# Attention ahead of a mixture of four dense branches: the first batch's head pairs one by one, a load moved, products of two pairs joined, and a planner's durations changed

## The chip, the cores and the metric

The kernel runs on one core of one Trainium2 chip. The metric is the device time of one execution in microseconds (us); below, "the median" is that of several runs. A core has a matrix engine (PE, whose weight loads are listed as PEld), a vector engine (DVE), a scalar engine (ACT), a general engine (POOL), and an engine that issues transfers (SP). They run side by side and wait for each other through semaphores; each executes its own list of instructions in order. Results of PE go to PSUM, which has eight banks of 128 x 512 numbers of four bytes; all else lies in SBUF.

## The reference

Everything is in float32. There are 8 batches, 8 heads, 576 rows and 64 columns to a head; the second half has N = 4608 rows, D = 512, four branches and F = 1024.

```python
kv = einsum('bhsd,bhse->bhde', k, v)          # 64 x 64 for each head
out = einsum('bhsd,bhde->bhse', q, kv)
x = out / sqrt(mean(out * out, -1) + 1e-6) * g_norm
x = x.transpose(0, 2, 1, 3).reshape(4608, 512)
p = domain_probs / (domain_probs.sum(-1, keepdims=True) + 1e-9)
result = sum(p[:, e:e + 1] * (maximum(x @ w1[e], 0) @ w2[e]) for e in range(4))
```

## The kernel before, in words

**Tiling.** The rows of x are cut into nine chunks of 512: the first 512 rows of each of the eight batches, and a ninth that gathers the 64 remaining rows of each batch. Branch e and chunk c make step s = 9e + c, 36 steps in all. A step's `up` makes the hidden layer (x times w1, then the maximum with 0), its `down` multiplies that by w2 and adds to the output. Both use Strassen-like schemes with seven products in place of eight (L868 for up; L1082 and, in most steps of branches 1 to 3, L1157 for down), so DVE, POOL and ACT form many sums and differences. The first step's `up` alone is plain (`up_plain`, L955): 32 products of 128 x 128 by 128 x 512, in four banks of kinds u1 and u2, two sweeps over the halves of the hidden layer.

**Attention of one batch** (`attention`, L570 to L741) goes by head pairs, four to a batch, two to a group. For a pair: q is loaded (two transfers of 128 KB), k and v (288 KB each); PE turns q by four transposes (L616), ACT copies it out (L621); PE multiplies k by v for both heads (L629: 12 products of 96 x 64 by 96 x 64, that is 24 steps on PE, since a float32 product takes two). For a group: ACT copies the k times v of two pairs (L638); PE multiplies q by it ("attend", L651: 64 steps, 64 x 64) into two raw banks, which are of kind db for batches 0 and 1 and of kind ab from batch 2 on. `scaled` (L518) then takes the rows' norm: ACT squares both banks (L533), DVE sums (L540), POOL scales and takes the power -1/2 (L547, L551), DVE multiplies the raw banks by that (L560). PE turns the resulting x (L670, four transposes to a pair), and ACT copies it out times `gcol`, the g_norm weights (L677). Products on 96 x 64 or 64 x 64 use half of PE's array. The 64 remaining rows of all four pairs follow in one go (L695, L712, L725, L735).

**What orders the work.** Nothing is in the program's order. Every operation is put into a `Plan` with a key (its due place in the sequence of steps), a cost (the engines that may do it, with a duration each; DVE or POOL for the sums of `combine`, L360), and what it reads and writes. `layout` (L81) then plays all engines against one clock: PE and SP take the first ready operation in order of key, the others the most urgent; buffers and banks are given out as they come free. A transfer's end is reckoned on a common bus (`bus`). Where PE could do nothing while the first key of its list is below 0, it is given a filler, two transposes of the identity (`idle`, L1289 to L1291). What comes out is one fixed list to each engine; the chip executes these lists with semaphores, whatever the durations turn out to be.

The g_norm weights are loaded by two transfers that stand in the code ahead of the planned ones (L1297), so they are the first on SP's queue. The SP order after them is: q, k, v of pairs 0 to 3 of batch 0, then the four quarters of w1 (512 KB each), then batch 1.

Of the kernel before, what the change touches and what calls it, by code (L numbers as in the profile page):

```python
# [9 lines left out]
ACT = mybir.ActivationFunctionType  # L10
# [24 lines left out]
class Plan:  # L35
# [45 lines left out]
    def layout(self, slots, later, idle, idle_banks, idle_until):  # L81
# [22 lines left out]
        busy = {e: 0.0 for e in todo}  # L104
        bus = port = 0.0
        lanes = [0.0] * self.LANES
        t = 0.0
# [123 lines left out]
def kernel(  # L231
# [104 lines left out]
    def pe(products, columns, passes=2):  # L336
        return {"PE": passes * products * (0.008 + 0.0008125 * columns) + 0.003}

    def dve(n):
        return {"DVE": 0.185 + 0.00104 * n}  # L340

    def act(n):
        return {"ACT": 0.19 + 0.00088 * n}

    def either(n):
        return {"DVE": 0.185 + 0.00104 * n, "POOL": 0.15 + 0.00225 * n}

# [170 lines left out]
    def scaled(key, name, raw, n, x, blocks):  # L518
# [36 lines left out]

        plan.add(key - 0.3, {"POOL": 2.1}, power, reads=[ss], writes=[ss, rt])
        for r in range(2):
# [12 lines left out]
    def attention(b, key, span, rem):  # L570
# [6 lines left out]
        at = lambda j: key + span * j / (NPAIR + 1)  # L577
        kv = [Buf("kvbd", f"kvc{b}_{g}") for g in range(2)]
        qTs = {}

# [23 lines left out]

        for g in range(2):
            kbank = Buf("ab", f"kv{b}_{g}")
            for o in range(2):
                hp = 2 * g + o
                kt, vt, qt = load_pair(hp)
                bank = Buf("ab", f"qT{b}_{hp}")  # L610
                qT = qTs[hp] = Buf("small", f"qT{b}_{hp}")

                def turn(eng, bank=bank, qt=qt):
                    for r in range(NR):
                        rs = slice(r * P, (r + 1) * P)
                        nc.tensor.transpose(bank.ap[:, rs], qt.ap[:, rs], ident[:])  # L616

                plan.add(at(hp), pe(4, P, 1), turn, reads=[qt], writes=[bank])
                plan.add(
                    at(hp), act(NT),  # L620
                    lambda eng, bank=bank, qT=qT: nc.scalar.activation(  # L621
                        out=qT.ap[:], in_=bank.ap[:], func=ACT.Copy),
                    reads=[bank], writes=[qT],
                )

                def key_values(eng, bank=kbank, kt=kt, vt=vt, o=o):
                    for j in range(KR):
                        for r in range(2):
                            nc.tensor.matmul(  # L629
                                bank.ap[r * D:(r + 1) * D, o * D:(o + 1) * D],  # L630
                                lhsT=kv_rows(kt)[:, r, j, :], rhs=kv_rows(vt)[:, r, j, :],
                                start=(j == 0), stop=(j == KR - 1), skip_group_check=True,
                            )

                plan.add(at(hp), {"PE": 0.87}, key_values, reads=[kt, vt], parts=[kbank])
            plan.add(
                at(2 * g + 1), act(P),
                lambda eng, bank=kbank, to=kv[g]: nc.scalar.activation(  # L638
                    out=to.ap[:], in_=bank.ap[:, 0:P], func=ACT.Copy),
                reads=[kbank], writes=[kv[g]],  # L640
            )
            raw = [Buf("ab" if b > 1 else "db", f"raw{b}_{g}_{r}") for r in range(2)]

            def attend(eng, raw=raw, g=g):
                for o in range(2):
                    for i in range(NR):
                        for c in range(2):
                            for r in range(2):
                                half = slice(r * D, (r + 1) * D)
                                at = i * P + c * D  # L650
                                nc.tensor.matmul(  # L651
                                    raw[r].ap[c * D:(c + 1) * D, (o * NR + i) * D:(o * NR + i + 1) * D],
                                    lhsT=qTs[2 * g + o].ap[half, at:at + D],
                                    rhs=kv[g].ap[half, o * D:(o + 1) * D],
                                )

            plan.add(
                at(2 * g + 1.4), {"PE": 1.0}, attend, reads=[qTs[2 * g], qTs[2 * g + 1], kv[g]],
                writes=raw,
            )  # L660
            x = Buf("big", f"xg{b}_{g}")
            scaled(at(2 * g + 1.4), f"{b}_{g}", raw, P, x, 2 * NR)
            for o in range(2):
                hp = 2 * g + o
                bank = Buf("ab" if b > 1 else "db", f"xT{b}_{hp}")

                def turn_x(eng, bank=bank, x=x, o=o):
                    for r in range(NR):
# [3 lines left out]

                plan.add(at(2 * g + 2 + 0.4 * o), pe(4, P, 1), turn_x, reads=[x], writes=[bank])
                xh = x_halves(b)[g]
                plan.add(
                    at(2 * g + 2 + 0.4 * o), act(NT),
                    lambda eng, bank=bank, xh=xh, kt=o: nc.scalar.activation(  # L677
                        out=xh.ap[:, kt * NT:(kt + 1) * NT], in_=bank.ap[:], func=ACT.Copy,
                        scale=gcol[:]),
                    reads=[bank], parts=[xh],  # L680
                )
# [26 lines left out]
        def attend_rem(eng):  # L708
            for hp in range(NPAIR):
                for r in range(2):  # L710
                    half = slice(r * D, (r + 1) * D)
                    nc.tensor.matmul(  # L712
                        rawr[r].ap[0:REM, hp * D:(hp + 1) * D],
                        lhsT=qTr.ap[half, hp * REM:(hp + 1) * REM],
                        rhs=kv[hp // 2].ap[half, hp % 2 * D:(hp % 2 + 1) * D],
                    )

        plan.add(at(NPAIR), {"PE": 0.55}, attend_rem, reads=[qTr] + kv, writes=rawr)
        xr = Buf("small", f"x{n}")
# [222 lines left out]
    def up_plain(s, e, c, key, span):  # L942
# [4 lines left out]
        for i in range(8):  # L947
            uh, a, u = i // 4, i // 2 % 2, i % 2
            bank = Buf("u1" if a == 0 else "u2", f"up{s}_{i}")
            for dh in range(2):  # L950
                w, low = corners[uh, dh]

                def product(eng, w=w, bank=bank, dh=dh, ut=2 * a + u):
# [7 lines left out]
                op = plan.add(  # L961
                    key + span * i / 8 - (1.1 if i < 4 and dh == 0 else 0.0), pe(2, NT), product,
                    reads=[w, low, xh[dh]], **({"parts": [bank]} if dh else {"writes": [bank]}),
# [23 lines left out]
    def result(s, e, c, base):  # L987
# [33 lines left out]
        def merge(key, src, ap, i, half, fresh):  # L1021
# [4 lines left out]
            if fresh and not again:  # L1026
                plan.add(
                    key, act(HN),
                    lambda eng: nc.scalar.activation(  # L1029
# [14 lines left out]
        def send(key, i):  # L1044
# [4 lines left out]
            def fn(eng):  # L1049
# [6 lines left out]
            plan.add(  # L1056
                key, {"POOL": 0.9 * len(where)} if e and not again else {"SP": 0.55 * len(where)},
                fn, reads=[part[i, 0], part[i, 1]] + ([was] if was else []), writes=[now], kb=256,
# [197 lines left out]


    attention(0, -2.0, 1.3, 0.1)
    sums_1 = weights_1(0, -2.5, 0.02, 0.3)
# [35 lines left out]
    with tc.manual_schedule(engines={ENG.PE, ENG.DVE, ENG.Activation, ENG.Pool, ENG.SP}):  # L1295
        for i in range(P // D):
            nc.sync.dma_start(out=gcol[i * D:(i + 1) * D, :], in_=g_norm.unsqueeze(1))  # L1297
        make_identity(nc, ident[:])
# [45 lines left out]
```

## Time and profile before

| | us |
|---|---|
| median of six runs (1741.33 to 1745.49) | 1742.67 |
| the profiled execution | 1740.68 |
| its span, first to last instruction | 1738.7 |

| stretch of the span | PE busy | DVE busy | ACT busy | POOL busy | DMA share |
|---|---|---|---|---|---|
| 0 to 29 us | 24.02 | 2.58 | 6.58 | 3.82 | 0.98 |
| 29 to 37 us | 8.00 | 3.51 | 1.09 | 5.43 | 1.13 |
| 37 to 60 us | 23.00 | 19.03 | 9.81 | 9.27 | 0.80 |
| 60 to 100 us | 40.00 | 29.26 | 19.86 | 25.92 | 0.74 |
| 100 to 200 us | 100.00 | 59.79 | 50.52 | 36.15 | 0.51 |
| 200 to 420 us | 220.00 | 116.89 | 108.07 | 71.92 | 0.41 |
| 420 to 1710 us | 1289.92 | 910.79 | 718.12 | 542.88 | 0.43 |
| 1710 to 1738.7 us | 24.04 | 9.24 | 2.98 | 5.82 | 0.43 |

The page's first part gives the busy time of each engine and the number of its instructions. "Busy" counts fillers as well as work, and ends of PE's instructions are modelled. A row of the waits view has the engine and tile that waited, its line, what it waited for, and then the total in us, the number of times and the longest. A line of the timeline has a start, a length, engine, line, what is written and read, shapes, how many instructions stand together, and in brackets the idle time ahead and who ended it. The chain of waits is followed back from the last instruction; its pieces follow each other without a gap, so their lengths add up to the span. Lines are those of the kernel before; L360 and the like are lines of helpers that issue many operations.

### The profile page before, as it was taken

The numbers are of one execution on the slowest core, as the hardware profiler recorded it, in microseconds if no ns is written. First come the engines' busy times: TensorE is split into PE (matmuls) and PEld (weight loads), VectorE is DVE, ScalarE is ACT, GpSimd is POOL, SyncE is SP. The second block draws the span as 40 slices with busy tenths as digits, with TensorE's granted clock in tenths as the row PEclk, the third lists the DMA queues.
The fourth block names the chain that finished last, engine by engine and source line by source line (L and its number), as shares of the span: only waits on it lengthen the run. The fifth ranks groups of instructions, "written<-read, shape, count | busy, mean of one in ns | idle before, by whom it ended". The sixth has DMA issues, their size and how long they took to land.

```text
span 1738.7 us, 37793 instructions
## 1 busy us (share of the span) xinstructions
PE 1729.0 (99%) x15080; PEld 1650.7 (95%) x15080; DVE 1151.1 (66%) x1745; ACT 917.0 (53%) x2234; POOL 701.2 (40%) x684
## 2 busy tenths in 40 slices
PE   8999999999999999999999999999999999999998
PEld 6699999999999999999999999999999999999998
DVE  2765554556574467777786567777786567777774
ACT  2454544454444455666655456666555446665662
POOL 2633343333333524333356524333345625333331
PEclk9999999999999999999999999999999999999999
DMA  9755544533333333444455434444456434444442
GB/s 229 242 177 159 174 143 128 150 135 127 146 125 107 103 97 105 110 110 110 133 159 134 110 97 110 110 110 110 108 158 160 110 98 110 110 110 109 109 100 49
DMA packets 148592, 220.89 MB, mean 127 GB/s; under 512 B 49600, under 2 KB 90816, under 8 KB 148416
## 3 DMA queue, kind: packets, MB, share of 16 engines
q1 hardware_dynamic: 133312, 191.21, 34.5%
q0 software_dynamic: 15104, 27.27, 11.0%
q8 instruction: 118, 1.93, 0.4%
q14 instruction: 58, 0.48, 0.1%
HBM read 145.30 MB, written 73.14 MB: 126 GB/s over the span
## 4 chain that ended last, share of the span: by engine, by line
PE 99%; DMA 0%; DVE 0%; issue 0%; SPq 0%; ACT 0%
PE u L868 45%; PE db L1082 17%; PE db L1157 16%; PE ab L1157 10%; PE ab L1082 4%; PE u L955 2%; PE ab L629 2%; PE ab L616 1%; PE ab L651 1%; PE ab L1291 1%; PE ab L670 1%; PE db L651 0%; PE ab L712 0%; DMA small<-in_q_dram 0%; PE db L670 0%; PE ab L695 0%
## 5 line engine op out<-in xcount | busy, mean ns | idle before, releaser
L868 PE MATMUL u<-xf,big 128*128 128x128 f32 x3536 | 509.3, 275 | 0.0
L360 DVE TENSOR_TENSOR big<-big,big 128x1024 f32<-128x1024 f32 (+1 forms) x420 | 462.2, 1112 | 56.0 <-ACT big L851 26.1
L868 PEld LDWEIGHTS u<-xf,big 128*128 128x128 f32 x3536 | 456.2, 192 | 4.3
L868 PE MATMUL u<-xf,w1y 128*128 128x128 f32 x2652 | 383.0, 276 | 0.0
L895 DVE TENSOR_TENSOR big<-u,snap 128x256 f32<-128x256 f32 x446 | 188.2, 422 | 257.3 <-PE u L868 192.8
L868 PEld LDWEIGHTS u<-xf,w1y 128*128 128x128 f32 x2652 | 342.1, 192 | 3.7
L887 ACT ACTIVATE snap<-u 128x256 f32<-128x256 f32 x490 | 187.5, 383 | 241.7 <-PE u L868 202.9
L1082 PE MATMUL db<-big,big 128*128 128x256 f32 x1192 | 280.4, 380 | 0.0
L1082 PEld LDWEIGHTS db<-big,big 128*128 128x128 f32 x1192 | 216.3, 190 | 24.5
L360 POOL TENSOR_TENSOR big<-big,big 128x256 f32<-128x256 f32 (+1 forms) x125 | 161.0, 1302 | 162.0 <-DVE big L360 62.1
L887 ACT ACTIVATE big<-u 128x256 f32<-128x256 f32 x446 | 170.1, 383 | 106.2 <-PE u L868 77.3
L360 POOL TENSOR_TENSOR big<-big 128x512 f32<-128x512 f32 (+1 forms) x75 | 90.9, 1213 | 161.6 <-DVE big L360 107.6
L851 ACT ACTIVATE big<-big 128x1024 f32<-128x1024 f32 x124 | 130.1, 1051 | 6.7 <-DVE big L360 4.8
L1157 PE MATMUL db<-big,big 128*128 128x128 f32 x788 | 113.0, 275 | 0.0
L1223 POOL TENSOR_TENSOR big<-big 128x512 f32<-128x512 f32 x19 | 24.1, 1268 | 217.9 <-DVE big L360 164.1
L1185 ACT ACTIVATE snap<-db 128x256 f32<-128x256 f32 (+1 forms) x168 | 59.9, 356 | 94.5 <-PE db L1157 88.1
L887 ACT ACTIVATE u<-u 128x256 f32<-128x256 f32 x245 | 91.0, 371 | 29.1 <-PE u L868 12.4
L1157 PEld LDWEIGHTS db<-big,big 128*128 128x128 f32 x788 | 100.3, 192 | 0.0
L1029 ACT ACTIVATE big<-db,p_all 128x256 f32<-128x256 f32 x90 | 42.6, 473 | 108.9 <-PE db L1082 108.9
L1052 POOL DMA_DIRECT2D out_dram<-big x98 | 88.5, 989 | 22.0 <-ACT big L1029 16.3
L1157 PE MATMUL db<-kv,big 128*128 128x128 f32 x624 | 88.6, 275 | 0.0
L1157 PE MATMUL ab<-kv,big 128*128 128x128 f32 x588 | 84.1, 275 | 0.0
(208 smaller groups left out, 2623.5 us busy)
## 6 DMA issues: line engine op xcount, KB each, us to landing
xf<-x SPq DMA_DIRECT2D x108, 512.0 KB, 3.5
out_dram<-big POOLq DMA_DIRECT2D x82, 256.0 KB, 5.3
xf<-x_h SPq DMA_DIRECT2D x81, 256.0 KB, 3.0
xf<-x SPq DMA_DIRECT2D x81, 256.0 KB, 3.1
x<-xf SPq DMA_DIRECT2D x36, 512.0 KB, 3.0
big<-in_moe_w_dram SPq DMA_DIRECT2D x28, 512.0 KB, 5.2
small<-in_q_dram SPq DMA_DIRECT2D x72, 128.0 KB, 3.9
kv<-in_k_dram SPq DMA_DIRECT2D x30, 288.0 KB, 3.3
```

The source lines that it names most:

```text
L360: lambda eng: adder(eng).tensor_tensor(out=out_(), in0=a(), in1=b(), op=op),
L629: nc.tensor.matmul(bank.ap[r * D:(r + 1) * D, o * D:(o + 1) * D], lhsT=kv_rows(kt)[:, r, j, :], rhs=kv_rows(vt)[:, r, j, :], start=(j == 0 ...
L851: lambda eng: nc.scalar.activation(out=b.ap[:], in_=b.ap[:], func=ACT.Relu),
L868: nc.tensor.matmul(ps.ap[:, u * P:(u + 1) * P], lhsT=w1f[e][m][mm][1]()[:, u * P:(u + 1) * P], rhs=views[m][mm][1](), start=(mm in (1, 5) ...
L887: lambda eng: nc.scalar.activation(out=where(), in_=ps.ap[:, 0:HN], func=ACT.Copy),
L895: lambda eng: nc.vector.tensor_tensor(out=block(whole, a, t), in0=src.ap[:, 0:HN], in1=add_.ap[:], op=ALU.add),
L955: nc.tensor.matmul(bank.ap[:], lhsT=two(w.ap[:])[:, kt, ut * P:(ut + 1) * P], rhs=two(xh[dh].ap[:])[:, kt, :], start=(dh == kt == 0), stop ...
L1029: lambda eng: nc.scalar.activation(out=cell(i, half), in_=ap(), func=ACT.Copy, scale=prob()),
L1052: nc.gpsimd.dma_start(out=dst, in_=cell(i)[parts, :], accum_op=ALU.add)
L1082: nc.tensor.matmul(ps.ap[:, 0:HN], lhsT=four(h[m])[:, kt // 2, t, kt % 2, :], rhs=w2f[e][m].ap[:, kt * HN:(kt + 1) * HN], start=(m in (1, ...
L1157: nc.tensor.matmul(ps.ap[:, o * P:(o + 1) * P], lhsT=b.ap[:, col:col + P], rhs=w2q[e][m][mm][1]()[:, kt, :], start=(mm in (1, 5) and o == ...
L1185: lambda eng: nc.scalar.activation(out=where(), in_=group_of(ps.ap), func=ACT.Copy),
```

## The change

- The eight banks and all products stay. In batch 0 the groups of attention are single pairs: four groups in place of two, each with its own copy of k times v, attend (32 steps), squares, sum, power (8 columns instead of 16), scaling, and turn. One raw bank of each is now of kind db, the other of kind u2. Batches 1 to 7 keep groups of two pairs.
- `key_values` is one operation for a group: the 24 steps of each of its pairs follow one another.
- The loads of g_norm become a planned operation (`load_gains`) with a key between those of pairs 1 and 2; the copies of batch 0's x wait for it.
- x is turned in ab banks in all batches (before: db for batches 0 and 1).
- `up_plain` puts the first half of the products of two banks ahead of their key, not of four.
- The planner's durations: DVE 0.155 in place of 0.185, ACT 0.155 in place of 0.19 (the part per column stays); POOL's power 0.3 + 0.37 for each block in place of 2.1; the first merge of an output cell 0.48 in place of 0.415; POOL's sends 1.0 in place of 0.9; k times v 0.73 a pair + 0.2, attend 0.5 a pair + 0.2, the remainder's attend 0.75 in place of 0.55. The common bus starts at 3.0 in place of 0.

The lines of the changed kernel are 4 to 18 higher from there on: L616 becomes L620, L629 L634, L638 L647, L651 L660, L670 L678, L677 L686, L955 L968, L868 L881, L1082 L1095, L1291 L1311.

```diff
-        bus = port = 0.0
+        bus, port = 3.0, 0.0
...
     def dve(n):
-        return {"DVE": 0.185 + 0.00104 * n}
+        return {"DVE": 0.155 + 0.00104 * n}
...
     def act(n):
-        return {"ACT": 0.19 + 0.00088 * n}
+        return {"ACT": 0.155 + 0.00088 * n}
...
-        plan.add(key - 0.3, {"POOL": 2.1}, power, reads=[ss], writes=[ss, rt])
+        plan.add(key - 0.3, {"POOL": 0.3 + 0.37 * blocks}, power, reads=[ss], writes=[ss, rt])
...
-        for g in range(2):
-            kbank = Buf("ab", f"kv{b}_{g}")
-            for o in range(2):
-                hp = 2 * g + o
+        groups = ((0,), (1,), (2,), (3,)) if b == 0 else ((0, 1), (2, 3))
+        for g, pairs in enumerate(groups):
+            n = f"{b}_{g}"
+            kbank = Buf("ab", f"kv{n}")
+            kv = Buf("kvbd", f"kvc{n}")
+            held = []
+            for o, hp in enumerate(pairs):
+                kvs[hp] = kv, o
                 kt, vt, qt = load_pair(hp)
+                held.append((kt, vt))
...
-                def key_values(eng, bank=kbank, kt=kt, vt=vt, o=o):
+            def key_values(eng, bank=kbank, held=held):
+                for o, (kt, vt) in enumerate(held):
                     for j in range(KR):
...
-                plan.add(at(hp), {"PE": 0.87}, key_values, reads=[kt, vt], parts=[kbank])
+            size = len(pairs)
...
+            plan.add(
+                at(pairs[-1]), {"PE": 0.73 * size + 0.2}, key_values,
+                reads=[t for ts in held for t in ts], writes=[kbank],
+            )
...
-            raw = [Buf("ab" if b > 1 else "db", f"raw{b}_{g}_{r}") for r in range(2)]
+            raw = [Buf(("db", "u2")[r] if b == 0 else "ab" if b > 1 else "db", f"raw{n}_{r}") for r in range(2)]
...
-                at(2 * g + 1.4), {"PE": 1.0}, attend, reads=[qTs[2 * g], qTs[2 * g + 1], kv[g]],
-                writes=raw,
-            )
-            x = Buf("big", f"xg{b}_{g}")
-            scaled(at(2 * g + 1.4), f"{b}_{g}", raw, P, x, 2 * NR)
-            for o in range(2):
-                hp = 2 * g + o
-                bank = Buf("ab" if b > 1 else "db", f"xT{b}_{hp}")
+                at(pairs[-1] + 0.4), {"PE": 0.5 * size + 0.2}, attend,
+                reads=[qTs[hp] for hp in pairs] + [kv], writes=raw,
+            )
+            x = Buf("big", f"xg{n}")
+            scaled(at(pairs[-1] + 0.4), n, raw, P, x, size * NR)
+            for o, hp in enumerate(pairs):
+                bank = Buf("ab", f"xT{b}_{hp}")
...
-                    reads=[bank], parts=[xh],
+                    reads=[bank] + ([gains] if b == 0 else []), parts=[xh],
...
-                    key + span * i / 8 - (1.1 if i < 4 and dh == 0 else 0.0), pe(2, NT), product,
+                    key + span * i / 8 - (1.1 if i < 2 and dh == 0 else 0.0), pe(2, NT), product,
...
+    gains = Buf(None, "gains", gcol)
+
+    def load_gains(eng):
+        for i in range(P // D):
+            nc.sync.dma_start(out=gcol[i * D:(i + 1) * D, :], in_=g_norm.unsqueeze(1))
+
+    plan.add(-2.85, {"SP": 1.1}, load_gains, writes=[gains], kb=1)
     attention(0, -2.0, 1.3, 0.1)
...
-        for i in range(P // D):
-            nc.sync.dma_start(out=gcol[i * D:(i + 1) * D, :], in_=g_norm.unsqueeze(1))
         make_identity(nc, ident[:])
```

## The prediction

> **What bounds the kernel now.** I read the page first, then the waits of PE, then PE in order of time over the first 40 us, then the chain of waits inside the attention stage.
>
> The page:
> ```profile
> span 1738.7 us, 37793 instructions
> PE 1729.0 (99%) x15080; PEld 1650.7 (95%) x15080; DVE 1151.1 (66%) x1745; ACT 917.0 (53%) x2234; POOL 701.2 (40%) x684
> ```
> PE is busy for all but 9.7 us. The waits view of PE, for the whole span, says where (us, times, longest):
> ```profile
> PE ab L1291 <- POOL ident masks.py:199: 1.3, 1, 1.3
> PE ab L616 <- DMA small<-in_q_dram: 1.3, 1, 1.3
> PE ab L1291 <- issue: 1.3, 1, 1.3
> PE ab L1291 <- ACT small L621: 0.7, 1, 0.7
> PE db L651 <- issue: 0.3, 1, 0.3
> ```
> All of these lie before 29 us; the rest is the end of the span, about 4.6 us after the last product. From 29 us on PE never waits. So only three things change the time: when PE stops doing filler, how much PE work there is, and any new PE wait. But busy is not useful: L1291 is filler (transposes of the identity that the planner puts where PE would idle). Lines from PE's timeline:
> ```profile
> 1.35 4.10 PE L1291 MATMUL ab<-ident 128*128 128x128 f32 x18 [1.35 <-POOL ident masks.py:199]
> 6.77 0.63 PE L616 MATMUL ab<-ident,small 128*128 128x128 f32 x4 [1.31 <-DMA small<-in_q_dram]
> 7.23 2.13 PE L1291 MATMUL ab<-ident 128*128 128x128 f32 x18
> ...
> 28.96 7.13 PE L955 MATMUL u<-big,big 128*128 128x512 f32 x16
> 35.94 1.04 PE L1291 MATMUL ab<-ident 128*128 128x128 f32 x8
> 36.81 1.04 PE L670 MATMUL db<-ident,big 128*128 128x128 f32 x8
> ```
> The last filler ends at 36.8 us, where the x of the last two head pairs is turned. After that PE runs useful work without a gap. The first 18 transposes take 4.10 us (0.213 each), the next 18 take 2.13 us with the last one's drain in it (0.109 each): PE starts at half speed.
>
> The chain of waits in the attention stage has a second cost (start, us, what):
> ```profile
> 122.90 1.73 PE db L1082 x8
> 124.63 0.89 PE u L868 x8
> 125.52 0.85 PE ab L629 x24
> 126.37 2.43 PE u L868 x20
> 128.80 0.44 PE ab L616 x4
> 129.24 0.85 PE ab L629 x24
> 130.09 1.53 PE u L868 x12
> ```
> Eight L868 cost 0.89 (0.1115 each), so 20 should cost 2.23 and 12 should cost 1.34. After a block of L629, which uses half of the array, they cost 0.20 more. Between starts of instructions I read the same: the step into a half-array block is 0.205 instead of 0.112 (0.094 more), its last step 0.1 longer, and the first step of the full-size work behind it 0.10 longer (0.057 if that is transposes). One such block between full-size work costs 0.29.
>
> **The change part by part**, against the profiled execution (1740.68 us, span 1738.7). That is 2.0 below the median of the six runs, 1742.67.
>
> Start-up. I take PE's order from the instruction lists of both programs.
> - Before the first q transpose there are now 30 filler transposes instead of 18. The g_norm loads leave the head of SP's queue (two issues, 1.23 us), so q lands near 5.4 instead of 6.63, but PE is still in its filler. By about 5.3 us 18 slow ones are done; 12 more at 0.109 end near 6.65 (earliest 6.5; 7.75 if all 30 run slow). Before: 6.77. So the 1.27 us that every load of pairs 0 and 1 gains buys 0.1.
> - From there to the turn of the last pair's x: filler 84 x 0.109 = 9.2; four q turns 1.75; twelve x turns 1.3; four k-times-v blocks at 0.85+0.094+0.057 = 4.0; four half-length attends at 0.73 = 2.9 (half of the 64 steps, the three penalties); four 512-column products (x16 in 6.9, so 0.86 each) 3.45. Sum 22.6, so the last x turn starts at 29.2.
> - Nothing waits in it: the k and v of pair 3 land at 20.2 in the old trace and are wanted at 20.4; for pair 3 the squares, sum, power and scaling end 4.5 us after attend (old, two pairs: 7.0, of it 2.9 the power and 1.22 the sum, both by width), and 6 us of PE work stand there. If that cover were gone, each us late is a us.
> - Before, this point was at 36.81. By then before had done four more products (3.45) and had four more transposes left (0.44), so after owes 3.0. **Gain 36.8 - 29.2 - 3.0 = 4.6.**
>
> Fewer changes of the array's shape. Counted in the lists after the start: 65 half-array blocks before, 62 of them entered from full-size work; now 52 and 46, since k times v of two pairs runs as one block in seven batches. 16 x 0.294 = 4.7, less three more joints of half-array blocks with each other at 0.1: **gain 4.4.** The work itself is the same instructions.
>
> What batch 1 pays. Its raw results still lie in the two db banks, and the list now shows the first L1082 product (into a db bank) only 1.72 + 0.7 + 3.1 = 5.6 us of PE work behind the second attend: two 512-column products, the remainder's attend, seven L868 pairs. The bank is free when DVE has scaled the raw result. In the old trace this took 9.0 us (66.87 to 75.84), and PE had other work there. The lines of POOL and DVE:
> ```profile
> 68.11 1.22 DVE L540 TENSOR_REDUCE ss<-big 128x16 f32<-128x1024 f32 x1 [0.88 <-ACT big L533]
> 70.82 2.90 POOL L551 TENSOR_TENSOR rt<-ss,mhalf 128x16 f32<-128x16 f32 x1
> 73.76 1.29 DVE L560 TENSOR_TENSOR big<-db,rt 128x512 f32<-128x512 f32 x2
> ```
> In the new lists POOL does a 1024-wide sum of the hidden layer (2.4) ahead of that power; it starts after the last relus, 2.75 behind the attend. 2.75 + 2.4 + 3.2 (power with its scaling) + 0.7 (first half of DVE's) = 9.1. So PE waits 9.1 - 5.6 = 3.5, and everything behind it on PE waits too. Bounds: 0.9 if POOL were free (1.24 + 1.22 + 3.2 + 0.7 + gaps = 6.5), 7 if DVE, 83% busy in this stage, comes one 1024-wide sum (1.1 to 2.2) later at both of its steps. I take 3.5: it agrees with the old 9.0. **Loss 3.5.** No other place in the lists has two L868 of one bank back to back.
>
> The other edits. g_norm now lands behind pair 1 (worst old landing there 6.1 us, so by 12.5; first wanted past 18): nothing; if late, the whole first copy of x. Raw results in a db and a u2 bank: the u2 banks are first wanted by products at 25 us or later, nothing. The planner's durations (DVE and ACT 0.03 shorter, POOL's power and sends longer) move 91 operations to DVE and 81 off POOL; DVE is 66% busy and PE does not wait for it past 29 us, so nothing, but see the last rival; bounds -1 to +10. The new start of the planner's DMA clock shows only in the 30 fillers.
>
> Sum: 4.6 + 4.4 - 3.5 = 5.5 faster. 1740.68 - 5.5 = 1735.2 for a profiled execution, **1737.2 for the median**.
>
> [...]
>
> **The rivals.**
> 1. Batch 1 does not make PE wait. For it: PE finds work in the old order wherever x is late. Against: PE's list is fixed, and the bank is the same. 1742.67 - 9.0 = 1733.7. Chance 0.15.
> 2. The start is slower and the batch-1 wait doubles: 30 slow fillers (-1.1), wait 7 instead of 3.5, since DVE took more of the work there. 1742.67 - 4.4 = 1738.3, and with two more us of DVE's lateness in batch 2, about 1740.5. For it: DVE 19.03 of 23 us busy from 37 to 60. Against: its queue has gaps of 1 to 2 us there. Chance 0.17.
> 3. Slower: in batches 2 to 7 the second half of x comes late. By the old list 18 us of PE work stand between the last turn of a batch's x and the first product that needs that half; by the new one 5.1 us. ACT's copy (0.68), two 1024-wide sums already in DVE's queue (2.3), the relu between them (1.05) and the first differences (about 1.1) are 5.1 together. The price is the lateness six times: from 0.9 us each the gain is gone; at 1.6 each it is 1742.67 - 5.5 + 9.6 = 1746.8. Against: the first product needs the copy alone, the first that needs a difference stands 9 us behind the turn. Chance 0.10.
> 4. The start does not do what it says, since PE is paced by its own filler: this is in the sum already (0.1 for loads that come 1.27 earlier).
>
> **How the numbers follow.** Forecast 0.58, rivals 0.15, 0.17, 0.10. The forecast's own range is 1735.5 to 1740.5 (wait 1.8 to 6). Eight in ten: from rival 1 (1733.5) to rival 2 with the upper bound of DVE's cost (1743). A difference of 0.2% (3.5 us) is about what a measurement can tell from no change: faster is below 1739.2, slower above 1746.2. Faster: 0.58 x 0.85 + 0.15 + 0.17 x 0.15 = 0.67; slower: 0.07 of rival 3 and 0.02 of the rest, 0.09; same 0.24.
>
> **What would show it.** The last filler ends near 29 us (29.2, with the x turn behind it), 114 fillers in all, the q turn at 6.6. In the chain, L629 in blocks of x48. A single PE wait of 3 to 4 us between 60 and 75 us, released by DVE L560 in its new line, and none in later batches. If the gain at the start is there and the wait too, the steps hold. A wait that comes back every 57 us would be rival 3; a q turn after 7.5 the slow opening; no wait near 65 rival 1.

## The result, and the profile after

| | before | after |
|---|---|---|
| median of the runs beside each other | 1741.76 us (36 runs, 1739.73 to 1745.49) | 1737.53 us (18 runs, 1736.52 to 1738.20) |
| ratio after / before | | 0.9975, 95% interval 0.9968 to 0.9981 |
| the profiled execution | 1740.68 us | 1737.52 us |
| its span | 1738.7 us | 1735.7 us |

The change makes the kernel 4.2 us faster; 1737.2 was predicted. The profiled executions differ by 3.2 only: that of before was 1.1 below its median, that of after stands on it. The accounts below explain the spans, whose difference is 3.0.

The page of the kernel after (engine, busy time, share, instructions):
```profile
span 1735.7 us, 37757 instructions
PE 1726.1 (99%) x15074; PEld 1649.1 (95%) x15074; DVE 1163.7 (67%) x1836; ACT 921.4 (53%) x2240; POOL 639.4 (37%) x603
```
PE is busy 2.9 us less than before, with six instructions fewer. The change of time is a change of PE's list and of what each step costs, as the prediction had it. Work has moved from POOL (701 to 639 us) to DVE (1151 to 1164).

Lines are now those of the changed kernel, as listed with the change; the second line of down products, L1157, has become L1170.

PE's start in its timeline (start, length, instruction, count; in brackets the idle time ahead of it and who ended it):
```profile
1.35 5.51 PE L1311 MATMUL ab<-ident 128*128 128x128 f32 x30 [1.35 <-POOL ident masks.py:199]
6.70 0.60 PE L620 MATMUL ab<-ident,small 128*128 128x128 f32 x4
...
27.71 1.91 PE L1311 MATMUL ab<-ident 128*128 128x128 f32 x16
29.46 0.60 PE L678 MATMUL ab<-ident,big 128*128 128x128 f32 x4
```
Thirty fillers stand ahead of the q turn at 6.70 (predicted 6.65). The last filler ends, and the last x turn of batch 0 starts, at 29.46 (predicted 29.2; 36.81 before). Nothing between them waits.

All waits of PE over the whole span (us in total, times, longest):
```profile
PE db L1095 <- DVE big L560: 2.1, 1, 2.1
PE ab L1311 <- POOL ident masks.py:199: 1.4, 1, 1.4
PE u L881 <- ACT snap L900: 0.6, 1, 0.6
PE u L881 <- ACT u L900: 0.5, 1, 0.5
PE db L1170 <- ACT snap L1198: 0.4, 1, 0.4
PE ab L678 <- ACT big L686: 0.2, 1, 0.2
```
The first line is the predicted wait: the first L1095 of batch 1, released by DVE's scaling of the raw result in the bank that it wants. The third and fourth stand just ahead of it, the sixth just behind it; these three were not predicted. No line has "times 6" or 7: nothing comes back in batches 2 to 7. The L1170 line lies near 1705 us.

The stage of batch 1, out of the timeline of all engines (the product behind the second attend starts at 63.13):
```profile
63.13 1.98 PE L968 MATMUL u<-big,big 128*128 128x512 f32 x4
...
64.37 1.22 DVE L540 TENSOR_REDUCE ss<-big 128x16 f32<-128x1024 f32 x1
65.62 2.35 POOL L360 TENSOR_TENSOR big<-big,big 128x1024 f32<-128x1024 f32 x1 [0.70 <-ACT big L982]
68.40 3.76 POOL L551 TENSOR_TENSOR rt<-ss,mhalf 128x16 f32<-128x16 f32 x1
72.19 1.29 DVE L560 TENSOR_TENSOR big<-db,rt 128x512 f32<-128x512 f32 x2 [0.99 <-POOL rt L551]
72.94 2.99 PE L1095 MATMUL db<-big,big 128*128 128x256 f32 x8 [2.09 <-DVE big L560]
...
78.05 1.89 PE L1095 MATMUL db<-big,big 128*128 128x256 f32 x8
```
DVE has the row sums by 65.6, but POOL makes a 1024-wide sum of the hidden layer ahead of the power, as the lists said, and the bank comes free 9.8 us behind the attend (predicted 9.1; the power took 3.76, not 2.9). The last number to look at is the 2.99 of the eight L1095: the next such groups, from 78.05 on, take 1.89. The windows view shows why (stretch, its length, busy time of PE, PEld, DVE, ACT, POOL with counts, then the granted clock, the DMA share and GB/s):
```profile
66.97:70.38 3.41, 2.84 (x22) 2.55 (x23) 3.41 (x6) 1.30 (x4) 3.24 (x3) 1.00 1.02 410
70.38:73.79 3.41, 1.32 (x8) 1.05 (x8) 2.42 (x4) 0.23 (x1) 3.24 (x3) 1.00 0.55 159
73.79:77.20 3.41, 3.41 (x14) 2.53 (x12) 1.24 (x4) 0.86 (x2) 2.19 (x4) 0.50 0.28 107
77.20:80.60 3.40, 3.21 (x22) 2.80 (x22) 1.63 (x5) 2.13 (x6) 0.00 (x0) 1.00 0.60 186
```
From 73.79 to 77.20 us PE has half its clock. The steps of L1095 in it are 0.427 apart instead of 0.216, those of the transposes 0.213 instead of 0.109: about 1.4 us that no wait shows, because PE counts as busy.

What all this costs can be read between two starts. From the product behind the attend (63.13) to the second group of L1095 (78.05) are 14.9 us. The same instructions take 8.9 at the pace that they have elsewhere in this trace: 1.9 for the four L968 and 0.6 for the L722, 3.2 for 28 L881, 1.7 for eight L1095, 1.4 for the three turns. So batch 1 pays 6.0. The waits of the list make 3.4 of it (2.1, 0.6, 0.5 and 0.2); the list counts idle time from the modelled end of an instruction, and from start to start it is more: the 0.52 ahead of the L881 at 66.89 is a step of 0.79 where the usual one is 0.112, and the first step behind it takes 0.213.

The joined k times v in the chain of waits (start, us, what), as predicted in blocks of x48:
```profile
135.79 0.89 PE u L881 x8
136.69 1.55 PE ab L634 x48
138.24 0.64 PE u L881 x4
```
Two blocks of x24 took 0.85 each; one of x48 takes 1.55, and the penalties around it (the 0.64 of the four L881 behind it, 0.45 at their usual pace, shows one) come once instead of twice.

### The profile page after: what moved, and what is told of

It is laid out like the page before. It is cut to its first block, busy times and chain, and to the rows that moved or that the text cites. A ratio compares the mean times of both kernels' runs of the same rounds, so it can differ in the third digit from the quotient of the medians.

```text
span 1735.7 us, 37757 instructions
## 1 busy us (share of the span) xinstructions
PE 1726.1 (99%) x15074; PEld 1649.1 (95%) x15074; DVE 1163.7 (67%) x1836; ACT 921.4 (53%) x2240; POOL 639.4 (37%) x603
## 4 chain that ended last, share of the span: by engine, by line
PE 99%; POOL 0%; ACT 0%; DVE 0%; issue 0%; POOLq 0%
PE u L881 44%; PE db L1095 17%; PE db L1170 16%; PE ab L1170 10%; PE ab L1095 4%; PE u L968 2%; PE ab L634 1%; PE ab L678 1%; PE ab L620 1%; PE ab L1311 1%; PE ab L660 1%; PE db L660 0%; POOL rt L551 0%; PE ab L722 0%; PE ab L704 0%; PE ab L738 0%
## 5 line engine op out<-in xcount | busy, mean ns | idle before, releaser
L360 DVE TENSOR_TENSOR big<-big,big 128x1024 f32<-128x1024 f32 (+1 forms) x457 | 482.8, 1071 | 42.3 <-ACT big L864 27.8
L881 PE MATMUL u<-xf,big 128*128 128x128 f32 x3392 | 491.9, 275 | 0.0
L881 PEld LDWEIGHTS u<-xf,big 128*128 128x128 f32 x3392 | 439.1, 192 | 3.7
L881 PE MATMUL u<-xf,w1y 128*128 128x128 f32 x2652 | 388.0, 276 | 0.0
L881 PEld LDWEIGHTS u<-xf,w1y 128*128 128x128 f32 x2652 | 344.4, 192 | 3.4
L1095 PE MATMUL db<-big,big 128*128 128x256 f32 x1176 | 278.6, 381 | 2.1 <-DVE big L560 2.1
L1095 PEld LDWEIGHTS db<-big,big 128*128 128x128 f32 x1176 | 213.2, 191 | 26.0 <-DVE big L560 2.3
L360 POOL TENSOR_TENSOR big<-big,big 128x256 f32<-128x256 f32 (+1 forms) x140 | 184.2, 1330 | 128.6 <-DVE big L360 44.0
L864 ACT ACTIVATE big<-big 128x1024 f32<-128x1024 f32 x135 | 141.9, 1051 | 7.4 <-DVE big L360 3.8
L360 POOL TENSOR_TENSOR big<-big 128x512 f32<-128x512 f32 (+1 forms) x57 | 67.0, 1176 | 134.0 <-DVE big L360 100.1
L1065 POOL DMA_DIRECT2D out_dram<-big x106 | 94.9, 966 | 51.9 <-ACT big L1042 32.7
L1170 PE MATMUL db<-big,big 128*128 128x128 f32 x760 | 108.3, 275 | 0.4 <-ACT snap L1198 0.4
L1170 PEld LDWEIGHTS db<-big,big 128*128 128x128 f32 x760 | 96.4, 192 | 0.6 <-ACT snap L1198 0.6
L547 POOL TENSOR_SCALAR ss<-ss 128x16 f32<-128x16 f32 (+2 forms) x26 | 6.4, 245 | 241.4 <-DVE ss L540 241.2
L1049 DVE SCALAR_TENSOR_TENSOR big<-db,p_all,big 128x256 f32<-128x256 f32 x74 | 35.7, 483 | 87.3 <-PE db L1095 85.7
L1170 PE MATMUL ab<-kv,big 128*128 128x128 f32 x624 | 89.1, 275 | 0.0
```

Of the source, the lines that this page charges most:

```text
L360: lambda eng: adder(eng).tensor_tensor(out=out_(), in0=a(), in1=b(), op=op),
L864: lambda eng: nc.scalar.activation(out=b.ap[:], in_=b.ap[:], func=ACT.Relu),
L881: nc.tensor.matmul(ps.ap[:, u * P:(u + 1) * P], lhsT=w1f[e][m][mm][1]()[:, u * P:(u + 1) * P], rhs=views[m][mm][1](), start=(mm in (1, 5) ...
L1049: lambda eng: nc.vector.scalar_tensor_tensor(out=cell(i, half), in0=ap(), scalar=prob(), in1=cell(i, half), op0=ALU.mult, op1=ALU.add,),
L1065: nc.gpsimd.dma_start(out=dst, in_=cell(i)[parts, :], accum_op=ALU.add)
L1095: nc.tensor.matmul(ps.ap[:, 0:HN], lhsT=four(h[m])[:, kt // 2, t, kt % 2, :], rhs=w2f[e][m].ap[:, kt * HN:(kt + 1) * HN], start=(m in (1, ...
```

## The experiments

My theory after the result: the start gives 4.35 (36.81 - 29.46 - 3.0 owed), the joined blocks about 3.6 to 3.9, and batch 1 takes back 3.4 of waits (the four of the list) and 1.4 of half clock. (The blocks and the waits turned out larger, by about the same amount; see below.) The rivals: that the planner's durations or the load order are the gain, that the blocks' penalties are hidden, that the half clock has another cause. Medians below are of 5 to 11 runs; the ratio is to the runs of the kernel before on the same chip. They were taken in three series: fill_wait2, split_kv, join_only and early_b1; the next four; durations_only and raw1_ab. The median of the kernel before was 1742.85, 1741.64 and 1742.74 in them, and 1741.76 beside the changed kernel, so a difference between medians of two series is uncertain by about 1 us; where a reading rests on less, the traces decide.

| kernel | median us (lowest to highest) | ratio to before, 95% interval |
|---|---|---|
| fill_wait2 | 1736.16 (1735.83 to 1736.81) | 0.9962 (0.9949 to 0.9974) |
| split_kv | 1737.32 (1736.62 to 1737.65) | 0.9967 (0.9954 to 0.9979) |
| join_only | 1739.01 (1736.96 to 1741.45) | 0.9979 (0.9970 to 0.9988) |
| early_b1 | 1736.80 (1735.67 to 1737.00) | 0.9963 (0.9951 to 0.9976) |
| join_from_2 | 1734.62 (1734.23 to 1735.11) | 0.9963 (0.9951 to 0.9976) |
| join_from_2_bus15 | 1733.31 (1732.79 to 1733.52) | 0.9955 (0.9943 to 0.9968) |
| groups_of_two | 1739.11 (1738.36 to 1740.68) | 0.9986 (0.9977 to 0.9995) |
| gains_first | 1737.94 (1736.73 to 1739.26) | 0.9981 (0.9972 to 0.9990) |
| durations_only | 1741.99 (1739.37 to 1744.03) | 0.9993 (0.9984 to 1.0001) |
| raw1_ab | 1738.46 (1738.03 to 1740.75) | 0.9973 (0.9964 to 0.9982) |

**fill_wait2: PE busy through the wait.** To the changed kernel, in the function that makes an `up` product:
```diff
...
+                    made_ups.append(mm)
+                    if len(made_ups) == 7:
+                        for _ in range(18):
+                            nc.tensor.transpose(ps.ap[:, 2 * P:3 * P], ident[:], ident[:])
```


> The changed kernel with 18 transposes of the identity (18 x 0.109 = 2.0 us) behind the seventh L881 product, into columns of its bank that nobody reads: PE is busy through the 2.1 us in which it waited for batch 1's db bank, and L1095 starts no sooner. My theory: the wait is only filled, so it is no gain by itself, but the half clock from 73.8 to 77.2 us does not come: 1.4 us below the changed kernel, 1736.1, with L1095 at 0.216 a step from the start. Rival 1: the half clock is set by something else than that idle time (the two waits of 0.5 and 0.6 ahead of it, or a fixed time): no difference, 1737.5, steps of 0.427 again. Rival 2: the transposes hold up what waits for the bank: slower by up to 2 us.

Measured: 1736.16, 1.4 below the changed kernel. Its windows over the same place, and PE's timeline with the fillers (L891) and the product behind them, which is L1101 here:
```profile
70.40:73.80 3.40, 3.27 (x26) 2.96 (x25) 2.35 (x4) 0.14 (x1) 3.23 (x3) 1.00 0.60 174
73.80:77.20 3.40, 3.01 (x20) 2.44 (x20) 1.22 (x3) 2.07 (x5) 2.11 (x4) 1.00 0.31 118
```
```profile
63.06 1.99 PE L974 MATMUL u<-big,big 128*128 128x512 f32 x4
...
70.60 2.13 PE L891 MATMUL u<-ident 128*128 128x128 f32 x18
72.86 1.99 PE L1101 MATMUL db<-big,big 128*128 128x256 f32 x8
...
76.56 1.89 PE L1101 MATMUL db<-big,big 128*128 128x256 f32 x8
```
The product starts at 72.86 as in the changed kernel (72.94): nothing is earlier, only the clock stays at 1.00 and eight steps take 1.99 instead of 2.99. From the product behind the attend to the second group are 13.5 us instead of 14.9. So the idle time caused the half clock, and its price is 1.4; the other 4.6 of batch 1's 6.0 are waits.

**split_kv: the join undone.** To the changed kernel, one operation for each pair:
```diff
...
-            plan.add(
-                at(pairs[-1]), {"PE": 0.73 * size + 0.2}, key_values,
-                reads=[t for ts in held for t in ts], writes=[kbank],
-            )
+            for o, ts in enumerate(held):
+                plan.add(
+                    at(pairs[o]), {"PE": 0.93},
+                    lambda eng, f=key_values, some=((o, ts),): f(eng, some=some),
+                    reads=list(ts), parts=[kbank],
+                )
```


> The changed kernel with k times v of each pair as an operation of its own again. In the lists there are 13 more half-array blocks (73 against 60), 3.9 us by the penalties that I read off the trace (0.094 + 0.1 + 0.1 each), and the first L1095 of batch 1 stands 8.8 us behind the second attend instead of 5.8. My theory: +3.9 for the blocks, and of batch 1's 4.8 all but about 0.5 goes: 1737.1, near the changed kernel, and 4.5 above the kernel with the earlier attention. Rival 1: the changes of shape cost nothing that lasts (hidden in the pitch of the work around them): 1733. Rival 2: the wait in batch 1 is not tied to the joined operation and stays: 1741.

Measured: 1737.32. PE's waits:
```profile
...
PE ab L740 <- ACT big L688: 0.5, 1, 0.5
PE db L1172 <- ACT snap L1200: 0.4, 1, 0.4
```
The wait at the product in batch 1 is gone, and so is the half clock (the granted clock is 1.00 in every window from 45 to 90 us), and yet the time is that of the changed kernel: what the join saves it had paid back in batch 1. The saving can be summed over the steps from start to start, as what the steps into, inside and right behind half-array blocks take beyond the usual pace. Half-array blocks are those that the traces mark 96\*64 or 64\*64, where full-size work has 128\*128; I count the turns of the remaining rows (64\*128) as such blocks too. Behind the last x turn of batch 0 that is 20.1 us for 61 blocks here and 15.2 for 46 in the changed kernel, 0.33 a block in both; in the kernel before it is 20.5 for 62.

**join_only: the join on the kernel before.** The same joined operation (from batch 1 on), with groups, loads and durations as before.
```diff
...
+                if b == 0 or o == 1:
+                    plan.add(
+                        at(hp), {"PE": 0.87 * len(held)}, key_values,
+                        reads=[t for _, *ts in held for t in ts], parts=[kbank],
+                    )
...
```


> The kernel before with one part of the change alone: k times v of two pairs as one operation in batches 1 to 7. In the lists 13 fewer half-array blocks (58 against 71), 3.6 us less; the fillers and the start are as before; the first L1082 of batch 1 stands 6.4 us of PE work behind the second attend (8.8 in the kernel before, where nothing waits). My theory: the join brings the batch-1 wait with it: -3.6 + 3.0 of wait + 1.4 of half clock = 0.8 above the kernel before, 1742.5 (1741 to 1743.5). Rival 1: the join is a plain gain and the wait comes from the pair-by-pair first batch: 1738.2. Rival 2: the join does nothing but move work about: 1741.8, with no wait and no fewer cycles.

Measured: 1739.01, ratio 0.9979, so 2.1 to 5.2 us below before: nearer to rival 1 than to my 1742.5. Two lines of its timeline (L616 is the q turn, L1089 the product):
```profile
74.01 0.65 PE L616 MATMUL ab<-ident,small 128*128 128x128 f32 x4 [0.34 <-DVE small L560]
...
80.94 1.99 PE L1089 MATMUL db<-big,big 128*128 128x256 f32 x8 [0.75 <-DVE big L560]
```
A wait at the same product is there, as I said, but of 0.75, and no half clock follows it (the granted clock is 1.00 from 80 to 90 us): with this order the bank was free 8.0 us behind the attend (72.96 to 80.94). The join makes the place tight; for the 2.1 of the changed kernel the rest of its order is needed as well. The profiled execution (1741.36) was one of the slowest of the eleven: it has 6.8 us of half clock at its start, from 21.3 us on (14 fillers from 25.80 on take 2.84 us, 14 from 29.35 on take 1.69).

**early_b1: batch 1's attention due sooner.** To the changed kernel:
```diff
-                attention(c + 1, s - 0.1, 0.8, s + 0.5)
+                attention(c + 1, s - (0.15 if c == 0 else 0.1), 0.8, s + 0.5)
```


> The changed kernel with one number more: batch 1's attention is due 0.05 of a batch earlier. In the lists the second attend of batch 1 then stands 9.0 us of PE work ahead of the first L1095 (5.8 in the changed kernel), and POOL's power of that attend stands ahead of the 1024-wide sum instead of behind it. My theory: the wait at that product (2.1 us, with two waits of 0.5 and 0.6 just before it) and the half clock behind it (1.4) both go, and the order is 0.4 shorter by itself: about 5 us below the changed kernel, 1732.5; if the x turns (8.1 us behind the attend) wait instead, up to 1734. Rival 1: x is late whatever the order, so that the wait moves to the x turn: within 1 us of the changed kernel, 1736.5 to 1738. Rival 2: the half clock has nothing to do with the wait: a stretch of it stays, and the time is 1734.

Measured: 1736.80; my 1732.5 to 1734 is wrong, rival 1 right. Its waits:
```profile
PE ab L678 <- DVE big L560: 1.5, 1, 1.5
...
PE ab L678 <- DVE small L560: 1.2, 1, 1.2
...
```
The product in the db bank waits no more, but the x turns do, the first by 1.5 (batch 1's first group), the second by 1.2 (it needs an ab bank that holds the raw rows of the remainder). The windows around the second one:
```profile
69.48:72.89 3.41, 1.67 (x13) 1.32 (x13) 3.41 (x7) 0.80 (x3) 3.24 (x4) 1.00 0.52 140
72.89:76.30 3.41, 3.41 (x13) 3.05 (x14) 2.47 (x5) 1.37 (x2) 1.23 (x3) 0.50 0.26 103
```
The half clock came again.

**raw1_ab: other banks for batch 1.** To the changed kernel:
```diff
-            raw = [Buf(("db", "u2")[r] if b == 0 else "ab" if b > 1 else "db", f"raw{n}_{r}") for r in range(2)]
+            raw = [Buf(("db", "u2")[r] if b == 0 else "ab", f"raw{n}_{r}") for r in range(2)]
```


> The changed kernel with batch 1's raw results in ab banks, as in the later batches, so that no L1095 needs their banks. In the lists the first use of an ab bank (a q turn, L620) stands only 2.9 us of PE work behind the second attend, and POOL's power stands ahead of its 1024-wide sum, so x and banks should be ready 6.5 to 7 us behind the attend. My theory: moving the banks only moves the wait: about 4 us at L620 or the x turn, and the half clock behind it for another 3.4 us (1.0 to 1.6 us); 1738, within 1 of the changed kernel. Rival 1: the db banks were the cause, and without them no wait is left: 1732.6. Rival 2: the wait is there but no half clock: 1736.5.

Measured: 1738.46. The product is free, and a q turn of the next batch waits in its place:
```profile
PE ab L620 <- DVE big L560: 2.7, 1, 2.7
```
```profile
68.37:71.78 3.41, 1.68 (x11) 1.18 (x10) 2.81 (x8) 0.77 (x2) 2.52 (x2) 1.00 1.21 246
71.78:75.20 3.42, 1.95 (x9) 1.71 (x10) 1.29 (x2) 0.60 (x1) 0.69 (x1) 0.50 1.04 350
75.20:78.61 3.41, 3.41 (x27) 2.95 (x28) 1.68 (x5) 2.34 (x4) 0.00 (x0) 0.50 0.30 122
```
The wait of 2.7 lies across two such stretches, and two run at half clock. The time came out as expected (1738); the wait was 2.7 and not 4, and the half clock 6.8 us long and not 3.4. This profile is of the slowest of the eleven runs (1740.75, 2.3 above the median), so the second stretch at half clock need not be in the others.

**join_from_2: the join without batch 1.** As split_kv, but only for batches 0 and 1:
```diff
...
+            parts = [tuple(enumerate(held))] if b > 1 else [((o, ts),) for o, ts in enumerate(held)]
+            for some in parts:
+                plan.add(
+                    at(pairs[some[-1][0]]), {"PE": 0.73 * len(some) + 0.2},
+                    lambda eng, f=key_values, some=some: f(eng, some=some),
+                    reads=[t for _, ts in some for t in ts], parts=[kbank],
+                )
```


> The changed kernel with k times v joined in batches 2 to 7 alone; batch 1 keeps one operation for each pair. In the lists: 62 half-array blocks (60 changed, 73 with no join at all), 2.9 us less PE work than with no join (which ran at 1737.3 without a wait in batch 1), and the first L1095 of batch 1 stands 8.5 us behind the second attend (8.8 with no join, 5.8 changed). My theory, that the join's 3.9 us were paid back by the wait and the half clock of batch 1: 1737.3 - 2.9 = 1734.4, no wait of PE over 0.6 between 50 and 80 us, no half clock after the start. Rival 1: the join's blocks are worth nothing in the later batches: 1737. Rival 2: the wait comes back at 8.5 (0.3 us less cover) with the half clock: 1736 to 1737.5.

Measured: 1734.62, 2.7 below split_kv (of another series) for 11 half-array blocks less, and 2.9 below the changed kernel, with every later batch joined as there. PE's waits:
```profile
...
PE u L884 <- ACT u L903: 0.6, 1, 0.6
PE ab L741 <- ACT big L689: 0.5, 1, 0.5
PE db L1173 <- ACT snap L1201: 0.4, 1, 0.4
```
Batch 1 still waits 1.0 in two pieces (1.6 from start to start), and the clock stays whole (1.000 over the span). split_kv has only the second of them, about 0.8 less, so the 11 blocks gave about 3.5 and not 2.7. The traces say the same: 16.6 us beyond the usual pace for 50 blocks here, 20.1 for 61 there, 0.32 for each block less. Against the changed kernel there are four blocks more, 1.3 us. So batch 1 cost the changed kernel the 2.9 gained here, these 1.6, and 1.3: 5.8, near the 6.0 read off its own trace.

**join_from_2_bus15: fewer opening fillers.** To the one before:
```diff
-        bus, port = 3.0, 0.0
+        bus, port = 1.5, 0.0
```


> The one before with the planner's clock of the loads started at 1.5 us instead of 3.0, which leaves 18 opening transposes instead of 30 (100 in all instead of 114). q then should land near 5.4 us and its turn start near 5.6 instead of 6.7. My theory, that the fillers pace the opening and the 1.27 us of the g_norm loads were only bought 0.1: now they count, about 1.0 us less, 1733.4. Rival 1: the loads of k and v behind q are late then and PE waits for them: no gain, 1734.4 or more. Rival 2: PE idles for q so that the clock stays at half longer: 1735.

Measured: 1733.31, 1.3 less, the fastest of all. PE's start and its one new wait:
```profile
1.35 4.06 PE L1314 MATMUL ab<-ident 128*128 128x128 f32 x18 [1.35 <-POOL ident masks.py:199]
5.25 0.60 PE L620 MATMUL ab<-ident,small 128*128 128x128 f32 x4
```
```profile
PE ab L634 <- DMA big<-in_v_dram: 0.7, 1, 0.7
```
The q turn starts at 5.25 without a wait: q was there, and in the changed kernel PE was in its filler. It is 1.45 sooner than there (1.55 sooner than in join_from_2); a wait of 0.7 for a v appears further on, and the last x turn starts at 28.58 instead of 29.56.

**groups_of_two: batch 0 like the others.** To the changed kernel:
```diff
-        groups = ((0,), (1,), (2,), (3,)) if b == 0 else ((0, 1), (2, 3))
+        groups = ((0, 1), (2, 3))
```
(and the raw banks of batch 0 are of kind db again)

> The changed kernel with batch 0 in groups of two pairs like the others. In the lists 188 fillers instead of 114 (8.1 us more) and 4 half-array blocks fewer, so 7.5 us more PE work; the first L1095 of batch 1 stands 13 us behind the second attend, so no wait there. My theory: 7.5 - 4.8 (wait and half clock of batch 1 gone) = 2.7 above the changed kernel, 1740.2; that is, the pair-by-pair start is worth 7.5 against this order. Rival 1: the start's gain came from the loads and not from the groups: at most 1733. Rival 2: the start of the changed kernel is worth nothing that lasts, since PE's later order makes up for it: 1737.5.

Measured: 1739.11, 1.6 above the changed kernel, 4.5 above join_from_2, which has no such wait either. Its last x turns of batch 0:
```profile
30.43 4.97 PE L1311 MATMUL ab<-ident 128*128 128x128 f32 x44
35.23 1.04 PE L678 MATMUL ab<-ident,big 128*128 128x128 f32 x8
```
They stand at 35.23 behind 44 fillers in a row, nearly where the kernel before had them (36.81). The start is the groups' doing, not the loads'. By the lists the difference to join_from_2 is 6.5 and that to the changed kernel 2.7 (7.5 less the 4.8); both came out lower. The opening has a part in it: here the 30 fillers took 4.86 us, 5.51 in the changed kernel and 5.61 in join_from_2. In join_from_2 the same turn starts at 29.56, 5.7 sooner, and its batch 1 then gives 1.6 back in waits.

**gains_first: the g_norm loads first again.** To the changed kernel:
```diff
...
-    plan.add(-2.85, {"SP": 1.1}, load_gains, writes=[gains], kb=1)
...
     with tc.manual_schedule(engines={ENG.PE, ENG.DVE, ENG.Activation, ENG.Pool, ENG.SP}):
+        load_gains(None)
```


> The changed kernel with the two g_norm loads at the head of SP's queue again; the rest as changed. My theory: q lands 1.2 us later, near 6.6, but 30 opening transposes keep PE until 6.7 anyway: 0 to 0.2 above the changed kernel, 1737.6. Rival: every load of batch 0 is 1.2 us later and each is waited for: 1738.8.

Measured: 1737.94, with 1736.73 to 1739.26 about the changed kernel's 1737.53: nothing that shows, as expected. PE's q turn was at 7.13, but no load held it: the 30 fillers ahead of it took 5.93.

**durations_only: the planner's durations on the kernel before** (the changed costs of `dve`, `act`, `either`, the power, the remainder's attend, the merge and the sends, and attend's 1.0 to 1.2; for example):
```diff
-        return {"DVE": 0.185 + 0.00104 * n}
+        return {"DVE": 0.155 + 0.00104 * n}
...
```


> The kernel before with the planner's durations of the change alone (no join, old groups, old load order). In the lists 0.2 us less PE work from the first q turn on (4 half-array blocks fewer, 16 fillers more), the first L1082 of batch 1 stands 11 us behind the second attend. My theory: the durations are nothing by themselves: 1741.6, within 1.5 of the kernel before. Rival 1: they are the gain (order and engines chosen better): 1737.5. Rival 2: work moved to DVE makes PE wait for it: 1744 or more.

Measured: 1741.99, ratio 0.9993 (0.9984 to 1.0001): nothing that shows. The 0.4 wait near the end comes with them (it is in the profile of every kernel that has the new durations and in neither without).

## Why the prediction was right, and where not

**The start: right.** Predicted gain 4.6, read off the trace 4.35 (last x turn at 29.46 instead of 29.2). That it comes from the groups shows in groups_of_two, where with groups of two this turn is at 35.23 though the loads are the new ones. That the 1.27 us of the loads would be bought only 0.1, because PE's own filler sets the pace, holds too: gains_first shows nothing, and with 18 fillers instead of 30 (join_from_2_bus15) the last x turn comes 1.0 sooner and the time falls by 1.3, where the kernel before, with 18 fillers and the old loads, waited 1.3 for q.

**Fewer changes of the array's shape: right, the term a sixth too small.** I took 16 entries from full-size work at 0.294 and got 4.4. The traces have these 16 (62 before, 46 after) at 0.33: 5.3. The experiment without the wait (join_from_2 against split_kv) gives 0.32 a block.

**Batch 1: the mechanism right, the price short.** The bank, the product, the releaser, the POOL sum ahead of the power and the place (a single wait of this kind, in the first batch behind the start) were as said. The 3.5 became 4.6. Up to the product they are 4.0: it starts 9.8 us behind the attend instead of 9.1, mostly because the power took 3.76 and not 2.9, and the PE work in between is 5.8 (the three terms of the prediction add up to 5.5, not 5.6, and a slow step behind a half-array block comes on top). The rest is a wait at an x turn behind it and slow first steps. What failed is the sentence "PE waits 9.1 - 5.6 = 3.5, and everything behind it on PE waits too": besides the size, it takes the work behind the wait at its old speed. That ran at half clock for 3.41 us, 1.4 more, a term that the prediction had at nothing. Shown by fill_wait2, where that alone is taken away.

**The rest.** The g_norm load and the durations at nothing: right within what was measured; the new durations come with the wait of 0.4 near 1705 us (0.5 from start to start), inside their bounds. For the banks of batch 0 there is only the trace, in which no wait names them. DVE's larger share brought no wait in later batches. That x is turned in ab banks, and the new order in `up_plain`, were not taken out one by one.

**The sum.** 4.35 + 5.3 - 4.6 - 1.4 - 0.5 = 3.15, against 3.0 in spans; the prediction had 5.5. So the profiled execution was predicted at 1735.2 and came out at 1737.52. That the predicted median is nonetheless within 0.4 is in part luck: the prediction set the profile of before 2.0 below the median of six runs, and over 36 runs it is 1.1. The medians differ by 4.2, more than the profiles, because the kernel before spreads: 1739.7 to 1745.5 against 1736.5 to 1738.2. One possible reason is its start, which waits for loads and for ACT. An idle time of PE near 20 us is 1.3 in its profile, 2.0 in that of durations_only and 2.6 in that of join_only, which have its groups and its loads; behind it the trace shows no half clock in the first, 3.4 us of it in the second and 6.8 in the third (mean granted clock 1.000, 0.999 and 0.998). The changed kernel has no wait there. That this differs between runs of one kernel, and makes up the 1.2, is not shown: over the 57 runs of the kernel before in the three series, the mean granted clock does not order the times (medians 1742.96 at 0.998, 1741.58 at 0.999, 1742.85 at 1.000).

**The rivals.** Rival 1 (no wait) and rival 3 (late x in each batch) are refuted by the waits. Rival 2's slow opening did not come (the q turn started at 6.70, not at 7.75); of its doubled wait (7) 4.6 came, and 1.4 of half clock. Its price was also added up wrongly: 4.4 leaves out the second half of the wait. 5.5 - 1.1 - 3.5 is 0.9, so the rival stood for 1741.8, not 1738.3, and for about 1744 with DVE's lateness.

The 8.0 us of join_only against the 9.8 of the changed kernel can be read off POOL's lines. Its wide sum starts 1.2 us behind the attend instead of 2.5, and its power takes 2.96 instead of 3.76; the scaling ahead of the power takes 0.25 more. What stays open is why the same power takes 2.9 in one place and 3.8 in the other.

## What to carry to other kernels

A wait on the engine that bounds the kernel is to be priced with what it does to the work behind it: here 2.1 us of idle time in one wait cost 1.4 more in clock, and filling them with useless transposes won that back. Two gains that each hold alone need not add: a joined operation shortens the cover of something else, and the sum has to be made at the place where they meet. And where a kernel fills its own start, look whether data or filler sets the pace before a load is moved.

## What the hardware did that I had not expected

**Half the clock behind a wait.** In the profile of after the granted clock is 1.00 from 5.52 us on, 0.50 from 73.79 to 77.20, and 1.00 again from there to the end of the work. The wait of 2.09 ahead of this ends at 72.94. Let a stretch be 3.41 us, as long as that one. In the stretch right ahead of a half clock PE was busy for 1.32 us (after, from 70.38), 1.67 (early_b1, from 69.48) or 1.68 (raw1_ab, from 68.37); in after the idle time was one gap of 2.09, in early_b1 two of 0.56 and 1.18. Behind stretches with 2.84 busy (after, from 66.97), 2.45 (early_b1, from 55.82) and 3.27 (fill_wait2, from 70.40) the clock stayed at 1.00, and so it did behind one with 2.10 in the kernel before, the first line here:
```profile
5.36:8.77 3.41, 2.10 (x20) 2.04 (x20) 0.00 (x0) 0.60 (x1) 0.00 (x0) 1.00 1.12 254
...
21.26:24.67 3.41, 2.72 (x17) 2.00 (x17) 1.29 (x2) 0.60 (x1) 0.28 (x1) 0.50 1.08 366
```
Two stretches that ran at half clock themselves were followed by a second one at half clock: the second line, from join_only, with 2.72 busy, and the one from 71.78 in raw1_ab, with 1.95. What decides between these cases is not shown.

**The opening differs in length.** In after the first steps of the opening transposes are 0.213 us apart up to 5.46, and those from 5.60 on 0.109. In the kernel before, 18 of them are 0.213 apart up to 5.03, and the next transposes, from 6.91 on, 0.109. PE had run nothing but transposes until then, in both. Where 30 of the same transposes open the program they last from 4.86 (groups_of_two) to 6.19 us (raw1_ab). That this is a part of the spread between runs of one kernel is a guess of mine: there is one profile of each kernel.
